# Held-back down products, more staging tiles, one conversion stream and a finer last norm in a fused attention and two-MoE kernel

## The chip, the cores and the metric

The kernel runs on 1 core of one Trainium2 chip. The metric is the device time of one execution in microseconds (us). Three timed runs of the kernel before gave 1191.64, 1191.96 and 1192.28 us; the median, 1191.96 us, is what a change is compared with. Times inside the kernel come from one profiled execution. PE is TensorE's matrix multiply, PEld its weight load, DVE is VectorE, ACT is ScalarE, POOL is GpSimd, and SP issues DMAs.

## What is computed

Three stages follow each other, on 6016 rows of 256 channels, all in float32:

```python
qn = q / (np.linalg.norm(q, axis=1, keepdims=True) + 1e-06)
kn = k / (np.linalg.norm(k, axis=1, keepdims=True) + 1e-06)
s = kn.transpose(0, 2, 1) @ qn / tau          # 256 x 256: attention over channels
a = softmax(s);  x = v @ a                    # 6016 x 256
h = np.maximum(x @ w_in, 0.0)                 # w_in 256 x 2048
x = h * h @ w_out                             # w_out 2048 x 256
xn = x / np.sqrt(np.mean(x * x, axis=-1) + 1e-06) * rms_g
g = xn @ w_gate;  val = xn @ w_val            # 256 x 1536 each
out = (g / (1 + np.exp(-g)) * val) @ w_out2   # 1536 x 256
```

## The kernel before

**Arithmetic.** A float32 operand is split into a high part (ACT, a copy that rounds) and a low part (DVE, a subtraction), and a product is three matmuls: high by high, low by high, high by low (`mm3`). The weights arrive in another number layout and are converted first: a `Call` scales halves on POOL and ACT (`a`, L142 and L145), then three DVE instructions put the bits together (`b0` L149, `b1` L153, `b2` L157), then `h` and `l` split the result.

**Stages.** The tokens lie in 12 blocks: 0 to 9 have 512 columns, 10 and 11 have 448. After the attention and the first weights (to 161 us), `mlp1` computes the first MoE for blocks 2 to 7, one block after another, 16 units a block: 6 matmuls up, relu and square on ACT and DVE, and 6 matmuls down that are held in `pending` until three units later. Blocks 8 and 9, and 10 and 11, are two pairs (4 and 5) for `mlp1_pair`: 8 groups of seven products of three matmuls each (A11, S1, S2, A12, S3, A22, S4), a scheme that needs seven products where a plain one needs eight. `mlp2` then does the second MoE for all six pairs the same way, 12 groups each.

**The pair stage, where most of the diff lies.** A group works in four PSUM banks. ACT copies a bank into the next one where a product adds on top of an earlier sum (`cp`, L1339 `bu` from `b0`, L1347 `bv` from `bu`), so a product may wait for ACT. Four results a group are relu'd and squared: for each, `square` makes a high part `sh` (`hi`, ACT, L1298), the full square (`full`, ACT L1302 or DVE L1304) and the low part (`lo`, DVE, L1307), and queues two down products (three matmuls each, lines 110 to 112, tiles `acc<-sh,wo_h`). They are put into the list `waiting` with the slot number from which they may go. Between the products there are eight calls of `down_slot` a group; a call issues what `pending` still holds from `mlp1`, and then the first down product of `waiting` that is due. `sh` lies in a rotating set of five buffers (`work`), and a group takes five. PE runs strictly in the order written, so a down product whose `sh` isn't ready stops the products behind it.

**Side work.** Beside the matmuls the kernel norms the finished blocks (`norm_steps`, `pair_norm`), splits them into seven operands and stores these in DRAM (`pair_steps`: `hi` L1038 on ACT, `lo` L1048 on DVE, a store from a staging tile after each), prepares the next pair's operands (`v_steps`), converts weights (`small_steps`, `stream`) and forms sums of `m` (`comb_steps`). In blocks 2 to 7 the tables `SKIP`, `ROWS` and `COMB` say which unit takes which step; in the pair stage and in `mlp2` a list `side` is taken off step by step by `aside`. Staging tiles are two buffers under the tag `ys`, for the last pair one `vt` and one `ys`. A step whose tile is still being stored waits, and with it everything behind it on ACT.

**Queues.** Nearly all DMAs go through SP's queue in the order written; `fetch` loads operands of `mlp2` back, `late_calls` load the last weights of w_out2 during `mlp2` and convert them, starting with the ACT step of L145.

Of the kernel before, what the change touches and what calls it, by code (L numbers as in the profile page):

```python
# [10 lines left out]
F32 = mybir.dt.float32  # L11
F32R = mybir.dt.float32r
# [16 lines left out]
def attn_moe_kernel(ctx: ExitStack, tc, q, k, v, tau, w_in, w_out, w_gate, w_val, w2, rms_g, out):  # L29
# [375 lines left out]
    def stream(cs, ahead):  # L405
# [8 lines left out]
        yield lambda: loads(ahead)  # L414
        for i, c in enumerate(cs):

            def bits(c=c):
                c.b0()
                c.b1()

            def whole(i=i, c=c):
                c.b2()
                if not c.keeps_raw:
                    loads(i + 1 + ahead)

            if i == 0:
                yield c.a
            yield from [bits, whole]
# [522 lines left out]
    def pair_norm(p):  # L951
# [64 lines left out]
        return [s1, s2, s2b, s3, s4, s5, s5b, s6(0), s6(1)]  # L1016

    def pair_steps(p, single=()):
# [3 lines left out]
        turn = []  # L1022
# [8 lines left out]
        def hi(i):  # L1031
            def f():
                if single:
                    st[i] = single[len(turn)][:, :, :n]
                    turn[:] = [] if turn else [0]
                else:
                    st[i] = xp.tile([P, 2, NB], F32R, tag="ys", name="xp", bufs=2)[:, :, :n]
# [15 lines left out]
        if single:  # L1053
            return sub, hi, lo

        def both(*fs):
# [5 lines left out]
            both(lo(6)),  # L1062
# [102 lines left out]
    def v_steps(p, into):  # L1165
# [11 lines left out]
        def tr(t, kk):  # L1177
            def f():
                if t == 0 and kk == 0:
                    st["t"] = vp.tile([P, KC, NB], F32, tag="vt", name="vt")[:, :, :n]  # L1180
                    st["a"], st["c"] = (place(k, F32)[:, :, :n] for k in (0, 1))
                    st["x"] = {
                        0: st["t"][:, 0], 4: st["t"][:, 1], 2: st["a"][:, 0], 6: st["a"][:, 1],
                        3: st["c"][:, 0], 1: st["c"][:, 1], 5: st["t"][:, 0],
                    }
# [54 lines left out]
    def through_dram(p):  # L1240

        count = [0]

        def into(i, n):
            if p not in v_dram:
                v_dram[p] = dp.tile([P, NC7, 2, NB], F32, tag=f"v{p}", name="vd")
            count[0] += 1
            t = place(6) if count[0] in (2, 4) else xp.tile([P, 2, NB], F32R, tag="ys", name="xp", bufs=2)
            t = t[:, :, :n]
# [19 lines left out]
    def mlp1_pair(p, ops, side, after_product, after_group):  # L1269
# [21 lines left out]
        def square(r, k, f, t, first, last):  # L1291
# [551 lines left out]
```

## Time and profile before

| | |
|---|---|
| timed runs, median | 1191.96 us (1191.64 to 1192.28) |
| the profiled execution | 1189.03 us, its span 1187.2 us |
| PE busy | 1137.5 us, 96% of the span, 5170 matmuls |
| PEld busy | 931.4 us, 78% |
| DVE busy, ACT busy | 777.5 us (65%), 789.9 us (67%) |
| POOL busy | 74.4 us (6%) |
| granted PE clock, mean | 0.993 |

The ends of matmuls are modelled in the profile: a matmul of 512 columns is shown with 389 ns, and the next one starts 227 ns after it when nothing is missing. So the busy share of PE says little about how dense it runs; the distance between starts, or the number of matmuls in a stretch, says it. A row in square brackets at the end of a timeline line is the engine's idle time before that instruction and what ended it.

### The profile page before, as it was taken

What the parts mean: (1) busy time and instruction counts of PE and PEld (TensorE: products, weight loads), DVE (VectorE), ACT (ScalarE), POOL (GpSimd) and SP (SyncE); (2) the same over time, 40 slices, a digit from 0 to 9 for tenths busy, and PEclk for the clock granted to TensorE, in tenths of its full rate; (3) what the DMA queues carried; (4) which work ended last, traced back from release to release, by engine and by line L of the source; (5) the groups of instructions that cost most, each with busy time, mean ns of one, the idle gap of its engine ahead of it and who ended that gap; (6) DMA issues with size and microseconds to landing.
All of it is one profiled execution on the core that took longest, in us unless ns stands there. A gap on an engine that the chain in (4) does not pass through costs nothing. (4 is left out here: it accounts for less than half of the span.)

```text
span 1187.2 us, 14551 instructions
## 1 busy us (share of the span) xinstructions
PE 1137.5 (96%) x5170; PEld 931.4 (78%) x5170; DVE 777.5 (65%) x1190; ACT 789.9 (67%) x1428; POOL 74.4 (6%) x106
## 2 busy tenths in 40 slices
PE   8999989999999998899888999999999999999997
PEld 7978878777778775667666778888888888888997
DVE  7998756688788775665653786655655655555655
ACT  7688768587788675666566776655655655655654
POOL 2421010210111000000000000000000000000000
PEclk9999999999999999999999999999999999999999
DMA  9533300363541310426034534202202201201101
GB/s 336 200 112 90 89 18 19 124 203 116 178 142 62 133 43 9 144 80 221 9 134 173 217 121 148 71 18 71 72 18 64 79 19 55 81 18 43 39 18 32
DMA packets 103033, 113.42 MB, mean 96 GB/s; under 512 B 50352, under 2 KB 71856, under 8 KB 102320
## 3 DMA queue, kind: packets, MB, share of 16 engines
q1 hardware_dynamic: 100688, 111.63, 28.3%
q10 hardware_dynamic: 2272, 0.85, 0.3%
q8 instruction: 41, 0.67, 0.2%
q14 instruction: 32, 0.26, 0.1%
HBM read 71.30 MB, written 41.16 MB: 95 GB/s over the span
## 5 line engine op out<-in xcount | busy, mean ns | idle before, releaser
L1414 PE MATMUL mm<-p,gv 128*128 128x512 f32 (+1 forms) x1188 | 304.1, 389 | 5.7 <-ACT mm L1456 4.7
L1414 PEld LDWEIGHTS mm<-p,gv 128*128 128x128 f32 x1188 | 222.3, 189 | 53.2 <-ACT mm L1456 6.3
L1505 DVE TENSOR_TENSOR sh<-hp,sh 128x512 fp32r<-128x512 f32 (+1 forms) x144 | 98.0, 681 | 144.7 <-ACT sh L1501 144.5
L111 PE MATMUL acc<-sh,wo_h 128*128 128x512 f32 (+1 forms) x384 | 155.4, 405 | 13.9 <-DVE sh L1307 11.3
L110 PE MATMUL acc<-sh,wo_h 128*128 128x512 f32 (+1 forms) x384 | 152.5, 397 | 9.9 <-ACT sh L1298 6.5
L112 PE MATMUL acc<-sh,wo_l 128*128 128x512 f32 (+1 forms) x384 | 150.0, 391 | 3.9 <-DVE wo_l L182 3.8
L1456 ACT COPY mm<-mm 128x512 f32<-128x512 f32 (+1 forms) x72 | 40.4, 562 | 168.6 <-PE mm L1414 163.6
L850 DVE TENSOR_TENSOR sh<-p,sh 128x512 fp32r<-128x512 f32 x128 | 92.1, 720 | 62.6 <-ACT sh L843 56.9
L110 PE MATMUL acc<-sh,w_h 128*128 128x512 f32 (+1 forms) x284 | 109.5, 386 | 0.0
L112 PE MATMUL acc<-sh,w_l 128*128 128x512 f32 (+1 forms) x284 | 109.5, 385 | 0.0
L111 PE MATMUL acc<-sh,w_h 128*128 128x512 f32 (+1 forms) x284 | 109.5, 385 | 0.0
L111 PEld LDWEIGHTS acc<-sh,wo_h 128*128 128x128 f32 x384 | 72.6, 189 | 43.9 <-DVE sh L1307 24.7
L110 PEld LDWEIGHTS acc<-sh,wo_h 128*128 128x128 f32 x384 | 72.5, 189 | 33.2 <-ACT sh L1298 14.3
L1501 ACT CAST sh<-hp 128x512 fp32r<-128x512 f32 (+1 forms) x144 | 88.9, 618 | 4.8 <-DVE hp L1515 2.8
L112 PE MATMUL mm<-p,m_l 128*128 128x512 f32 x224 | 87.8, 392 | 0.4 <-DVE m_l L774 0.4
L838 ACT ACTIVATE p<-mm 128x512 f32<-128x512 f32 x128 | 75.6, 591 | 18.7 <-PE mm L112 18.2
L110 PE MATMUL mm<-p,m_h 128*128 128x512 f32 x224 | 87.8, 392 | 0.2 <-ACT ns L929 0.2
L111 PE MATMUL mm<-p,m_h 128*128 128x512 f32 x224 | 87.5, 391 | 0.0
L112 PEld LDWEIGHTS acc<-sh,wo_l 128*128 128x128 f32 x384 | 72.7, 189 | 16.9 <-DVE wo_l L182 5.1
L1414 PE MATMUL mm<-xs,gv 128*128 128x512 f32 (+1 forms) x324 | 82.5, 381 | 0.0
L1489 DVE TENSOR_TENSOR hp<-mm,sg 128x512 f32<-128x512 f32 (+1 forms) x72 | 48.9, 680 | 42.9 <-PE mm L1414 42.7
L1414 PEld LDWEIGHTS mm<-xs,gv 128*128 128x128 f32 x324 | 60.8, 188 | 10.2
(245 smaller groups left out, 2072.5 us busy)
## 6 DMA issues: line engine op xcount, KB each, us to landing
xd<-xp SPq DMA_DIRECT2D x70, 256.0 KB, 2.1
p<-xd SPq DMA_DIRECT2D x58, 256.0 KB, 4.0
gv<-gvd SPq DMA_DIRECT2D x5, 1792.0 KB, 14.8
gvd<-gp SPq DMA_DIRECT2D x15, 512.0 KB, 3.1
raw<-in_moe_w_out_dram SPq DMA_DIRECT2D x10, 512.0 KB, 3.8
out_dram<-ot SPq DMA_DIRECT2D x40, 128.0 KB, 2.3
qraw<-in_q_dram SPq DMA_DIRECT2D x13, 384.0 KB, 7.2
qraw<-in_k_dram SPq DMA_DIRECT2D x13, 384.0 KB, 7.3
```

The costliest lines, as they stand in the source:

```text
L110: nc.tensor.matmul(o, wh, xh, start=start, stop=False)
L111: nc.tensor.matmul(o, wh, xl, start=False, stop=False)
L112: nc.tensor.matmul(o, wl, xh, start=False, stop=stop)
L838: nc.scalar.activation(out=r, in_=o, func=AF.Relu)
L850: nc.vector.tensor_tensor(out=sl, in0=s, in1=f32(sh), op=ALU.subtract)
L1414: nc.tensor.matmul(bank, c[:, hl, a, fs], x, start=start and j == 0, stop=j == 2, skip_group_check=not start)
L1456: cp(out=bu, in_=b0)
L1489: dve(out=h21, in0=bv, in1=sg1, op=ALU.mult)
L1501: nc.scalar.copy(out=parts[t][0], in_=x)
L1505: dve(out=pl, in0=x, in1=f32(ph), op=ALU.subtract)
```

## The change

The pair stage and the tables change, no matmul is added or removed:

- `square` takes a `lag`, and its down products are due `lag` slots later (3, 2, 3 and 4 for the four squares of a group; 0 before). `cp(out=bu)` goes ahead of the square left over from the group before, and the norm's matmul (`takes_bank`) ahead of two slots, in `mlp2` too.
- `staged(...)` gives `pair_steps` and `v_steps` tiles in turn: `ys, p0, ys, p1` (blocks 5 and 7, pair 5), `ys, p6, ys` (pair 4), `vt, ys` with both `ys` buffers (last pair), and two `ys` as before only in block 3. So that `p0` and `p1` are free for it, `v_steps` takes them later and the operands of `mlp2`'s first pair are fetched at group 6 of pair 5, not at group 1.
- The two conversion streams become one (`w2_calls + gv_calls`, two loads ahead), in which `b0`, `b1` and `b2` are one step; the tables spread the steps anew, and block 7 takes its steps at other units.
- `pair_norm`'s first step becomes two; the last pair's list starts with three steps of the norm, and the conversion of late weights comes fourth, where it was second.

```diff
-        def s1():
-            st["w"] = vp.tile([P, 2, NB], F32, tag="vraw", name="w") if last else place(2, F32)
-            st["q"] = xp.tile([P, 2, NB], F32, tag="ys", name="q", bufs=2)
-            for d, x in enumerate((st["w"], st["q"])):
-                nc.scalar.activation(out=halves(x), in_=both(d), func=AF.Square)
+        def s1(d):
+            def f():
+                if d == 0:
+                    st["w"] = vp.tile([P, 2, NB], F32, tag="vraw", name="w") if last else place(2, F32)
+                    st["q"] = xp.tile([P, 2, NB], F32, tag="ys", name="q", bufs=2)
+                nc.scalar.activation(out=halves(st["wq"[d]]), in_=both(d), func=AF.Square)
+
+            return f
...
+    def staged(*tags):
+
+        turns = cycle(tags)
+
+        def tile():
+            t = next(turns)
+            if t[0] == "p":
+                return place(int(t[1]))
+            pool, k = (xp, 2) if t == "ys" else (vp, 1)
+            return pool.tile([P, 2, NB], F32R, tag=t, name="xp", bufs=k)
+
+        return tile
...
-                waiting.extend((slots["n"], down(f, t, d, st["h"], st["l"], first, last)) for d in range(KC))
+                due = slots["n"] + lag
+                waiting.extend((due, down(f, t, d, st["h"], st["l"], first, last)) for d in range(KC))
...
+            cp(out=bu, in_=b0)
             if old:
                 old[0]()
                 old[1](False)
                 old[2]()
-            cp(out=bu, in_=b0)
...
-            hi, full, lo = square(rx[:, 0], 0, f0, 0, first, False)
+            hi, full, lo = square(rx[:, 0], 0, f0, 0, first, False, 3)
...
+            if side and getattr(side[0], "takes_bank", False):
+                side.pop(0)(b0)()
             down_slot()
             down_slot()
-            if side and getattr(side[0], "takes_bank", False):
-                side.pop(0)(b0)()
             aside()
-            hi, full, lo = square(rx[:, 1], 1, f1, 1, first, False)
+            hi, full, lo = square(rx[:, 1], 1, f1, 1, first, False, 2)
...
-            hi, full, lo = square(ry[:, 0], 0, f1, 0, False, last)
+            hi, full, lo = square(ry[:, 0], 0, f1, 0, False, last, 3)
...
-            left.append(square(ry[:, 1], 1, f0, 1, False, last))
+            left.append(square(ry[:, 1], 1, f0, 1, False, last, 4))
...
-    conv = chain(small_steps(), stream(gv_calls, NRAW - 1))
-    conv2 = stream(w2_calls, 1)
+    conv = chain(small_steps(), stream(w2_calls + gv_calls, NRAW - 1))
...
-                if g == 1:
-                    for i in ORDER[:2]:
-                        fetch(0, i, ops0)
                 if g == NF1 // 2 - 2:
                     assert not side, len(side)
-                    fetch(0, 1, ops0)
+                    for i in ORDER[:3]:
+                        fetch(0, i, ops0)
...
     side = []
+    side += pair_side[:3]
+    del pair_side[:3]
     for i in range(max(len(rows_steps), len(pair_side))):
-        side += pair_side[i : i + 1] + rows_steps[i : i + 1]
+        side += rows_steps[i : i + 1] + pair_side[i : i + 1]
```

What this does to the order is seen on the engines (line numbers of the changed kernel are those of its own file: L1321 there is L1316, L1302 there is L1298). First PE, in the first group of pair 4 (`vr,m_h` are the products A12 and, later, A22; `vr,c3` is S3; `acc<-sh` are down products of the group's own squares), before:

```order
L1316 MATMUL mm_4002<-vr_3792,m_h_758 128x512
L110 MATMUL acc0_4056<-sh_4052,wo_h_91 128x512
L111 MATMUL acc0_4056<-sh_4052,wo_h_91 128x512
L112 MATMUL acc0_4056<-sh_4052,wo_l_92 128x512
L1316 MATMUL mm_4005<-vr_3949,c3_3622 128x512
L1316 MATMUL mm_4005<-vr_3949,c3_3623 128x512
L1316 MATMUL mm_4005<-vr_3949,c3_3622 128x512
L110 MATMUL acc1_4065<-sh_4052,wo_h_91 128x512
```

and now:

```order
L1321 MATMUL mm_4002<-vr_3785,m_h_758 128x512
L1321 MATMUL mm_4005<-vr_3924,c3_3622 128x512
L1321 MATMUL mm_4005<-vr_3924,c3_3623 128x512
L1321 MATMUL mm_4005<-vr_3924,c3_3622 128x512
L1321 MATMUL mm_4005<-vr_3970,m_h_758 128x512
L1321 MATMUL mm_4005<-vr_3970,m_l_759 128x512
L1321 MATMUL mm_4005<-vr_3970,m_h_758 128x512
L110 MATMUL acc0_4073<-sh_4050,wo_h_91 128x512
```

Three slots of this first group stay empty, and the first down products move behind A22; from there on every slot is filled, with down products that are older. In a later group of pair 4 ACT's rows name the squares (`sh<-p3` is first the square of A12's result, then that of S3's), before:

```order
L1351 ACTIVATE p3_3999<-mm_4279 128x512
L1298 ACTIVATE sh_4323<-p3_3999 128x512
L1358 COPY sh_4313<-mm_4282 128x512
L1038 CAST xp_4343<-xst_3783 128x512
L1298 ACTIVATE sh_4346<-p3_3999 128x512
```

and now:

```order
L1356 ACTIVATE p3_3999<-mm_4271 128x512
L1302 ACTIVATE sh_4315<-p3_3999 128x512
L1363 COPY sh_4305<-mm_4274 128x512
L1048 CAST xp_4335<-xst_3821 128x512
L1302 ACTIVATE sh_4338<-p3_3999 128x512
```

and PE's rows of the same group show which of them is read behind A22, before:

```order
L1316 MATMUL mm_4282<-vr_3990,m_l_759 128x512
L1316 MATMUL mm_4282<-vr_3990,m_h_758 128x512
L110 MATMUL acc0_4083<-sh_4346,wo_h_91 128x512
L111 MATMUL acc0_4083<-sh_4346,wo_h_91 128x512
L112 MATMUL acc0_4083<-sh_4346,wo_l_92 128x512
```

and now:

```order
L1321 MATMUL mm_4274<-vr_3970,m_l_759 128x512
L1321 MATMUL mm_4274<-vr_3970,m_h_758 128x512
L110 MATMUL acc0_4073<-sh_4315,wo_h_91 128x512
L111 MATMUL acc0_4073<-sh_4315,wo_h_91 128x512
L112 MATMUL acc0_4073<-sh_4315,wo_l_92 128x512
```

Behind A22 the down product of the newest square (`sh_4346`) stood; now that of the square before it (`sh_4315`) stands there, and the newest one moves to the next group's first slots. Third, ACT at the end of `mlp2`'s first group and in its second (`w<-xst` and `q<-xst` are the norm's first step, `pu<-pu` the late weights' conversion, `mm<-mm` the copies that products need), before:

```order
L975 ACTIVATE w<-xst 128x896
L975 ACTIVATE q<-xst 128x896
L145 ACTIVATE pu<-pu 128x512
L1456 COPY mm<-mm 128x512
L1501 CAST sh<-hp 128x512
L1512 ACTIVATE sg<-sg 128x512
```

and now:

```order
L975 ACTIVATE w<-xst 128x896
L975 ACTIVATE q<-xst 128x896
L1461 COPY mm<-mm 128x512
L1506 CAST sh<-hp 128x512
L1517 ACTIVATE sg<-sg 128x512
L1476 COPY mm<-mm 128x512
L1477 COPY pu<-mm 128x512
L1506 CAST sh<-hp 128x512
L1481 ACTIVATE sg<-mm 128x512
L1485 COPY pu<-mm 128x512
L145 ACTIVATE pu<-pu 128x512
L1461 COPY mm<-mm 128x512
```

The conversion `pu<-pu` stood right behind `q<-xst`, ahead of the copy `mm<-mm` of the second group; now that group's copies come first.

## Rows read from the trace of the kernel before

**Rows 1.** Stretches: us, busy time (x count) of PE, PEld, DVE, ACT, POOL; clock, DMA.

```profile
161.27:439.14 277.87, 270.84 (x1167) 217.63 (x1166) 207.77 (x316) 214.36 (x380) 36.48 (x44) 0.99 0.33 109
439.14:545.00 105.86, 93.80 (x369) 67.97 (x368) 66.43 (x106) 65.64 (x117) 0.00 (x0) 0.98 0.26 92
545.00:638.06 93.06, 82.80 (x364) 66.88 (x362) 54.30 (x87) 57.23 (x108) 0.00 (x0) 0.98 0.26 95
638.06:699.79 61.73, 56.37 (x236) 44.22 (x235) 41.73 (x68) 43.12 (x79) 2.04 (x4) 0.97 0.50 194
699.79:1092.70 392.91, 392.53 (x1730) 323.68 (x1729) 228.35 (x345) 235.96 (x445) 0.65 (x1) 1.00 0.19 60
...
1103.00:1173.00 70.00, 70.00 (x346) 64.48 (x345) 40.79 (x68) 40.90 (x86) 0.00 (x0) 1.00 0.06 16
```

**Rows 2.** Waits of weight loads, 439.14 to 638.06: total us, times, longest.

```profile
PEld acc L111 <- DVE sh L1307: 24.7, 46, 1.4
PEld acc L110 <- ACT sh L1298: 14.3, 19, 2.0
PEld mm L1316 <- ACT mm L1339: 3.8, 3, 2.7
PEld mm L1316 <- ACT mm L1347: 2.5, 2, 2.1
```

**Rows 3.** Timeline of PE, pair 4: start, us, instruction, count, idle before.

```profile
503.67 0.84 PE L1316 MATMUL mm<-vr,c 128*128 128x512 f32 x3
504.51 0.49 PE L110 MATMUL acc<-sh,wo_h 128*128 128x512 f32 x1
505.40 0.50 PE L111 MATMUL acc<-sh,wo_h 128*128 128x512 f32 x1 [0.40 <-DVE sh L1307]
```

**Rows 4.** Timeline of ACT in the same group.

```profile
503.19 0.60 ACT L1351 ACTIVATE p<-mm 128x512 f32<-128x512 f32 x1 [0.28 <-PE mm L1316]
503.82 0.63 ACT L1298 ACTIVATE sh<-p 128x512 fp32r<-128x512 f32 x1
```

**Rows 5.** Timeline of DVE in the same group.

```profile
504.65 0.69 DVE L1307 TENSOR_TENSOR sh<-p,sh 128x512 fp32r<-128x512 f32 x1
```

**Rows 6.** A stretch of pair 4's first group, columns as in rows 1.

```profile
454.00:457.00 3.00, 3.00 (x8) 2.31 (x8) 0.99 (x2) 0.86 (x3) 0.00 (x0) 0.50 0.00 0
```

**Rows 7.** Waits of ACT for DMAs over the whole span.

```profile
ACT xp L1038 <- DMA xd<-xp: 21.8, 13, 3.5
ACT raw L145 <- DMA raw<-in_moe_w_out_dram: 7.8, 1, 7.8
```

**Rows 8.** Timeline of PE: single waits in blocks, pairs and the start of `mlp2`.

```profile
219.27 0.49 PE L110 MATMUL acc<-sh,wo_h 128*128 128x512 f32 x1 [1.09 <-ACT sh L843]
...
411.92 0.50 PE L110 MATMUL acc<-sh,wo_h 128*128 128x512 f32 x1 [1.38 <-ACT sh L846]
...
426.56 0.37 PE L925 MATMUL mm<-ns,mean_w 128*128 128x16 f32 x2 [1.20 <-DVE ns L919]
...
491.03 0.96 PE L1316 MATMUL mm<-vr,c 128*128 128x512 f32 x3 [1.64 <-ACT mm L1347]
...
596.64 0.47 PE L1316 MATMUL mm<-vf,ch 128*128 128x448 f32 x1 [2.34 <-ACT mm L1339]
...
645.40 3.09 PE L1414 MATMUL mm<-p,gv 128*128 128x512 f32 x12 [0.67 <-ACT pu L1480]
652.12 3.85 PE L1414 MATMUL mm<-p,gv 128*128 128x512 f32 x9 [3.64 <-ACT mm L1456]
```

**Rows 9.** Timeline of ACT at the late weights' first conversion.

```profile
650.92 0.67 ACT L145 ACTIVATE pu<-pu 128x512 int32<-128x512 uint32 x1 [3.88 <-DMA pu<-in_moe_w_out_dram]
```

**Rows 10.** Groups of DVE, 161.27 to 439.14: count, busy us, mean ns, idle before.

```profile
L153 DVE CUSTOM_DVE_ANT_0 dg<-raw,dg 128x1024 uint16<-128x1024 uint16 x13 | 9.0, 692 | 0.4
L157 DVE SCALAR_TENSOR_TENSOR dg<-raw,dg 128x512 int32<-128x512 int32 x13 | 8.8, 678 | 0.0
L149 DVE TENSOR_SCALAR dg<-dg 128x512 int32<-128x512 int32 x13 | 5.9, 451 | 0.5 <-POOL dg L142 0.5
```

More of the change, by code (lines that the diff above doesn't have):

```diff
@@ L1 @@
 from contextlib import ExitStack
-from itertools import chain
+from itertools import chain, cycle
 import concourse.bass as bass
@@ L412, in loads, with first @@
                 done[0] += 1
-        yield lambda: loads(ahead)
+        def first():
+            upto("h", len(calls))
+            upto("l", len(calls))
+            loads(ahead)
+        yield from [first, lambda: None, cs[0].a]
         for i, c in enumerate(cs):
-            def bits(c=c):
-                c.b0()
-                c.b1()
             def whole(i=i, c=c):
-                c.b2()
+                c.b()
                 if not c.keeps_raw:
                     loads(i + 1 + ahead)
-            if i == 0:
-                yield c.a
-            yield from [bits, whole]
+            yield whole
             hl = c.hl_steps()
@@ L1032, in f @@
             def f():
[L1033 to L1037, printed above, removed]
+                st[i] = stage()[:, :, :n]
                 nc.scalar.copy(out=st[i][:, 0], in_=xst[p][:, i, :n])
@@ L1179, in f @@
                 if t == 0 and kk == 0:
[L1180 to L1185, printed above, removed]
+                    x = vp.tile([P, KC, NB], F32, tag="vt", name="vt")[:, :, :n]
+                    st["x"] = {0: x[:, 0], 4: x[:, 1], 5: x[:, 0]}
+                if t == 1 and kk == 0:
+                    a, c = (place(k, F32)[:, :, :n] for k in (0, 1))
+                    st["x"].update({2: a[:, 0], 6: a[:, 1], 3: c[:, 0], 1: c[:, 1]})
                 x = st["x"][SLOT[t][kk]]
@@ L1240, in through_dram @@
     def through_dram(p):
-        count = [0]
+        tile = staged("ys", "p6", "ys", "p6", "ys", "ys", "ys")
         def into(i, n):
@@ L1246, in into @@
                 v_dram[p] = dp.tile([P, NC7, 2, NB], F32, tag=f"v{p}", name="vd")
[L1247 to L1249 removed]
+            t = tile()[:, :, :n]
             return t[:, 0], t[:, 1], lambda: nc.sync.dma_start(out=v_dram[p][:, i, :, :n], in_=f32(t))
@@ L1289, in down, with square @@
             return g
-        def square(r, k, f, t, first, last):
+        def square(r, k, f, t, first, last, lag):
             st = {}
@@ L1481, in group @@
             add(out=h22, in0=bh, in1=w, op=ALU.add)
+            if side and getattr(side[0], "takes_bank", False):
+                side.pop(0)(b0)()
             down_slots()
             down_slots()
-            if side and getattr(side[0], "takes_bank", False):
-                side.pop(0)(b0)()
             if f:
@@ L1684, in attn_moe_kernel @@
         if b == CONV[-1]:
-            left = [len(list(x)) for x in (conv, conv2, cstep)]
-            assert left == [0, 0, 0] and state["b"] == len(calls) == state["l"], left
+            left = [len(list(x)) for x in (conv, cstep)]
+            assert left == [0, 0] and state["b"] == len(calls) == state["l"], left
     assert not spill
@@ L1708, in after_group @@
             if g == 0:
-                side.extend((pair_norm(p - 1) + pair_steps(p - 1) if p > FIRST else []) + ([] if last else v_next[2:]))
+                side.extend((pair_norm(p - 1) + pair_steps(p - 1, staged("ys", "p0", "ys", "p1")) if p > FIRST else []) + ([] if last else v_next[2:]))
             if not last and g == NF1 // 2 - 2:
@@ L1727, in attn_moe_kernel @@
         ops1 = nxt
-    stage = [pool.tile([P, 2, NB], F32R, tag=t, name="xp", bufs=k) for pool, t, k in ((vp, "vt", 1), (xp, "ys", 2))]
-    sub, hi, lo = pair_steps(NP - 1, stage)
     silu_table()
```

40 lines of the change are left out of this document (13 added, 27 removed).

## The prediction, made before the change was run

> **What bounds the kernel now.** Read the stretches first [rows 1]. From 699.79 to 1092.70 us, inside `mlp2`, 1730 matmuls of 512 columns start in 392.91 us: 0.2271 us each, with no wait; for 448 columns 346 take 70.0 us, 0.2023 each. These are the price of a matmul when PE never waits, and with them the other stretches show what PE loses. Blocks 2 to 7 hold 6 x 192 = 1152 matmuls: 277.87 - 261.6 = 16.2 us lost. Pair 4 holds 8 x 45, plus 18 down products left by block 7, less 12 that run over: 366 x 0.2271 = 83.1, so 105.86 - 83.1 = 22.7 lost. Pair 5: 12 x 0.2271 + 348 x 0.2023 = 73.1 of 93.06, 19.9 lost. The start of `mlp2`, 220 of 512 and 12 of 448: 52.4 of 61.73, 9.3 lost. (The counts of the rows are a few higher, for matmuls that reach over an edge and the norm's tiny ones.) So PE bounds nearly everything, and 68.1 us are holes that can be closed; what lies before 161 us isn't touched.
>
> Here a page reads differently. PE's busy column leaves only 12.1 and 10.3 us idle in the two pairs, 22.3 against the 42.6 counted above [rows 1]. The Trainium skill (Perfetto Trace Analysis, Identifying the Most-Contended Engine) calls matmul busy share a poor measure because pipelined matmuls mislead in the trace, and wants the share of weight loads instead. That share is 323.68 of 392.91, 82.4%, in the dense stretch and 64.48 of 70.00, 92.1%, for 448 columns; at these the loads of the pairs, 67.97 and 66.88, would take 82.5 and 72.6 us, 43.8 us less than they do. By the busy column the pairs could give 20 us less than I forecast; the trace sides with the page.
>
> **What the holes in the pairs are.** The waits of the weight loads name them [rows 2]: 24.7 us for the low part `sh` of DVE L1307, 14.3 for the high part of ACT L1298, and only 3.8 and 2.5 for ACT's copies of banks. So 39.0 of 45.7 us, some 36 of the 42.6, are down products that stand on PE before their square is done. One group shows how [rows 3 to 5]: S3 starts at 503.67 and takes 3 x 0.227; the down product behind it, due at 504.35, starts its first matmul at 504.51 and its second at 505.40. The square it needs came from A12's result: relu at 503.19, high part at 503.82, low part from 504.65. A12 had ended one down product before S3, at 502.99, so to that second matmul the chain takes 2.4 us; PE has six matmuls, 1.36 us, to do meanwhile.
>
> **The part that holds down products back.** With lags of 3, 2, 3, 4 and eight slots for eight products a group, the order settles so: the square of A12 is used behind A22, 15 matmuls or 3.4 us after A12's end (2.4 needed); that of S3 in the next group's first slot, behind 21 matmuls after S3 or 4.8 us; the two others 24 or more matmuls after their products. In a group with no side work nothing is left to wait for. I check that the engines can follow: in pair 4 DVE has 66.43 and ACT 65.64 us of work for a dense 83.1 us (80 and 79%), in pair 5 54.30 and 57.23 for 73.1 [rows 1]. No engine becomes the bound on average. What stays: the first group of pair 4, where three slots are empty and S3 and A22 follow A12 without cover. ACT then has two copies of block 7's results, relu, high part and the copy behind S3, five times about 0.6 us [rows 4], some 3.2 us with hand-overs where PE has 1.36: 1.8 us lost. The clock may fall there too: in the same group before, behind two waits on squares, it stood at 0.50 (1.2 GHz) from 454.00 to 457.00, and eight matmuls took 0.2 us longer each, 1.6 us [rows 6]; half of that is counted. Five groups a pair carry side steps; counted from the order at 0.6 to 0.7 us an instruction [rows 4, 5], they come to 7 to 9.7 us on the fuller engine, against 10.2 of matmuls in pair 4 and 9.1 in pair 5; no row shows such a group at full speed. Bounds are 0, as in groups without, and 2 us each; I take 0.5, nearer to the first, since a copy has 2 us of cover. Pair 4 keeps 1.8 + 0.8 + 2.5, with the rounding up 5.5, pair 5 2.5: 8 of 42.6 stay, 34.6 gained.
>
> On the fall of the clock the Trainium skill (Perfetto Trace Analysis, Matmul Optimizations) says that TensorE scales with its utilization and wants matmuls back to back in batches. That speaks against leaving slots empty; the rows above show such a fall in this very group already. With it in full the sum is 0.8 us worse, without it 0.8 us better.
>
> **The part that stages in more tiles.** ACT waited 13 times, 21.8 us in all, for a store out of a staging tile [rows 7], while the tile's next user comes one or two steps later. Three of these waits reached PE: at 411.92 in block 7 (1.38 us idle before a high part, then a low part, then matmuls at the low clock; by the starts 4.1 us over the dense price), at 491.03 (1.64 idle) and at 596.64 (2.34, then nine matmuls at the low clock) [rows 8]. The last two are within the 42.6. With three or four tiles a tile's next user comes two or more steps later than now, and the wait is covered. Behind the wait in block 7 stood the norm, and the 1.20 at 426.56 (1.4 with the next matmul) [rows 8] goes with it, as far as a step moved by one unit lets it. Block 3 keeps two tiles.
>
> **The conversions.** The other ACT wait on a DMA, 7.8 us [rows 7], is the first of the rows of w_out2: loaded one step ahead behind a store on SP; PE lost 2.3 us after it, by 1.09 idle at 219.27 [rows 8] and smaller waits around it. In the single stream it is loaded two steps ahead with no store in front. Block losses named so far: 4.1 + 1.4 + 2.3 = 7.8 of 16.2. The remaining 8.4 comes from units with too many steps at once, and the tables only shuffle these. Fewer steps means L149, L153 and L157 in one unit, 0.45 + 0.69 + 0.68 = 1.8 us on DVE where 1.1 and 0.7 stood in two, 13 times [rows 10], and behind them in DVE's order waits the next unit's low part. PE reads it three units (8.2 us) later, so a single such clump is covered; two engines late at once are not. The 8.4 could become 3 or 17; I take 8.0. Gain 8.2.
>
> **The last norm.** At 652.12 PE had waited 3.64 us, and with the low clock after it lost 5.7, for a copy on ACT that stood behind L145 [rows 8]. L145 had waited 3.88 us for its load, which landed at 650.92 [rows 9]. Now L145 stands behind the second group's copies. The first group's 41 matmuls, dense, end at some 647.1, the second group's S3 21 matmuls or 4.8 us later, and the copy behind it near 652.6, after the landing. The first group lost another 0.67 idle at 645.40 [rows 8] behind S3, where now two held products stand as cover. 9.3 becomes 2.6: gain 6.7. Fetching the first operands at group 6 leaves two groups, 18 us, for them: nothing. Splitting the norm's first step adds no instruction.
>
> **Sum.** 34.6 + 8.2 + 6.7 = 49.5. On the profiled execution's own 1189.03 that is 1139.5; the median of the runs lies 2.9 above that execution, so 1142.5.
>
> **Rivals.**
> *The waits move to ACT and DVE.* Both are in order, and a denser PE brings their work closer. For it: ACT is at 79% and each group has several hand-overs. Against: the dense stretch of `mlp2`, the same scheme with products held two slots, waits for nothing at 60% ACT. Half of the pairs' holes, 21 us, would stay, and the blocks' 16.2 too: 1142.5 + 13 + 8.2 = 1163.7. Chance 0.12.
> *The clumped conversions cost more than the tiles save.* Each of 13 clumps holds the next low part by 0.7 us and more; if each passes 1.2 us on to PE, 15.6 is added to blocks that gain nothing: 1142.5 + 8.2 + 15.6 = 1166.3. For it: the 8.4 us that full units cost already. Against: three units of cover. Chance 0.07.
> *It doesn't do what it says.* The products are moved, but what they wait for moves with them, because the squares start later behind the copies. Then the 36 us stay, and only tiles, conversions and norm give: 1142.5 + 36 - 8 = 1170. Against: cp and squares keep their places within a few 0.6 us steps. Chance 0.03.
> *Slower: the held products keep `sh` occupied.* Five buffers, five taken a group: each square takes the buffer of the same square a group earlier. If a buffer were still held, the high part on ACT would wait, and in order behind it the copies that products need. At one product and one down, 1.36 us, for each of four squares in 16 groups, 87 us: 1229.5. It decides once a held product stands behind the point of reuse; the closest, A22's square, is freed 12 matmuls (2.7 us) before that. Chance 0.03.
>
> **How the numbers follow.** The forecast has 0.75 and its own range, from the bounds above, is 1131 (pairs keep 2, blocks 3) to 1160 (pairs 18, blocks 16). The range 1131 to 1163 takes in that and the nearer part of the first rival and leaves some 2 in 10 out. Faster by over 0.2% (2.4 us, about what a measurement of this kernel can tell) 0.96, slower 0.03, within 0.01.
>
> **What would show it.** Pair 4 some 88 us long and pair 5 some 76; waits of weight loads for `sh` near zero; no wait over 2 us of ACT for a staging store beyond block 3; blocks 2 to 7 near 270; L145 late in `mlp2`'s second group and no half clock there. It is wrong if groups without side work stay over 10.4 us, or if ACT's copies become the waits.

## The result, and the profile after

The changed kernel takes **1135.73 us** (median of 4 runs, 1134.87 to 1137.26); the kernel before, run beside it, 1192.12 (1191.64 to 1195.30). The ratio is 0.9523, with a 95% interval of 0.9504 to 0.9542. The prediction was 1142.5 with a range of 1131 to 1163, so the time fell inside it, 6.8 us under the forecast. The profiled execution took 1137.26 us, its span 1135.3.

In the code after, the lines that matter have moved a little: the pairs' products are L1321 (L1316 before), the squares' high part L1302 (L1298), the low part L1311 (L1307), the two bank copies L1340 and L1352 (L1339, L1347), the copy behind S3 L1363 (L1358), the staging copy L1048 (L1038), the products of `mlp2` L1419 (L1414), their first copy L1461 (L1456).

The stretches that answer to [rows 1], in the same order and columns: blocks 2 to 7, pair 4, pair 5, the start of `mlp2`, and its dense part.

```profile
157.62:426.72 269.10, 266.04 (x1167) 219.62 (x1166) 207.91 (x315) 216.81 (x378) 31.93 (x41) 0.99 0.34 115
426.72:511.27 84.55, 83.09 (x363) 67.40 (x362) 65.78 (x105) 64.32 (x118) 0.15 (x1) 1.00 0.29 103
511.27:588.05 76.78, 74.97 (x363) 67.62 (x362) 54.04 (x87) 55.57 (x107) 0.00 (x0) 1.00 0.34 125
588.05:649.80 61.75, 59.49 (x255) 46.34 (x254) 45.31 (x72) 45.46 (x84) 2.36 (x4) 1.00 0.54 206
649.90:1040.00 390.10, 390.10 (x1721) 322.17 (x1720) 226.02 (x341) 233.93 (x442) 0.97 (x1) 1.00 0.19 59
```

Pair 4 went from 105.86 to 84.55 us, pair 5 from 93.06 to 76.78, with nearly the same busy time on DVE and ACT as before (ACT 1.3 and 1.7 us less): PE has all but stopped waiting for these two engines. Six matmuls of pair 4, 1.4 us, now run behind it, and six of pair 5 run in the start of `mlp2`. The dense part costs what it did: 390.10 us over 1721 matmuls is 0.2267 each.

The waits of the weight loads over both pairs, 426.72 to 588.05 (what waited, for what: total us, times, longest), against 24.7, 14.3, 3.8 and 2.5 us in [rows 2]:

```profile
PEld mm L1321 <- ACT sh L1363: 2.0, 3, 1.6
PEld mm L1321 <- ACT mm L1340: 2.0, 2, 1.7
PEld mm L1321 <- ACT mm L1352: 1.1, 2, 0.7
PEld acc L111 <- DVE sh L1311: 0.9, 1, 0.9
```

The down products' waits for squares are gone but for one. And ACT's waits for stores out of staging tiles over the whole span, 21.8 us in [rows 7]; the wait of L145 for the rows of w_out2, 7.8 us there, no longer appears:

```profile
ACT xp L1048 <- DMA xd<-xp: 5.1, 7, 1.4
```

To compare many kernels I use one measure on each one's trace: over all matmuls of 512 or 448 columns in a stretch, how much later the next matmul starts than 0.2271 us (512) or 0.2023 us (448) after this one, summed. That is PE's loss, idle time and slow clock together. Distances behind smaller matmuls are left out, so the first row holds nothing of the attention (to 61.8 us). The start of `mlp2` is the same 253 matmuls in every kernel.

| PE's loss, us, in | before | after | change |
|---|---|---|---|
| ahead of block 2 (to 157.62 us; before: to 161.27) | 6.2 | 2.5 | -3.7 |
| blocks 2 to 7 | 15.2 | 6.2 | -9.0 |
| pair 4 | 22.6 | 2.7 | -19.9 |
| pair 5 | 20.0 | 3.6 | -16.4 |
| start of `mlp2` | 9.5 | 4.9 | -4.6 |
| behind it | 0.4 | 1.7 | +1.3 |
| sum | 73.9 | 21.6 | -52.3 |

The span became 51.9 us shorter, so this table holds the whole difference. Two of its rows weren't in the prediction: the first and the last.

### The profile page after: what moved, and what is told of

The parts are those of the page before. It is cut to its first block, busy times and chain, and to the rows that moved or that the text cites. A ratio compares the mean times of both kernels' runs of the same rounds, so it can differ in the third digit from the quotient of the medians.

```text
span 1135.3 us, 14564 instructions
## 1 busy us (share of the span) xinstructions
PE 1115.5 (98%) x5170; PEld 934.6 (82%) x5170; DVE 778.1 (69%) x1190; ACT 789.9 (70%) x1428; POOL 70.9 (6%) x106
## 4 chain that ended last, share of the span: by engine, by line
PE 83%; DVE 5%; ACT 5%; DMA 2%; issue 2%; POOL 1%; SPq 0%; DVEq 0%; ACTq 0%; POOLq 0%
PE mm L1419 28%; PE acc L110 12%; PE acc L112 12%; PE acc L111 12%; PE mm L1321 6%; PE mm L110 4%; PE mm L111 4%; PE mm L112 4%; POOL rows L569 1%; DMA qraw<-in_k_dram 1%; DMA rraw<-in_v_dram 1%; PE mm L761 1%; DMA xd<-xp 1%; ACT sh L842 0%; ACT p L841 0%
## 5 line engine op out<-in xcount | busy, mean ns | idle before, releaser
L1419 PE MATMUL mm<-p,gv 128*128 128x512 f32 (+1 forms) x1188 | 303.4, 388 | 2.0 <-ACT mm L1461 1.6
L1419 PEld LDWEIGHTS mm<-p,gv 128*128 128x128 f32 x1188 | 221.4, 188 | 49.7 <-ACT mm L1461 3.0
L1461 ACT COPY mm<-mm 128x512 f32<-128x512 f32 (+1 forms) x72 | 40.4, 562 | 171.9 <-PE mm L1419 144.5
L111 PE MATMUL acc<-sh,wo_h 128*128 128x512 f32 (+1 forms) x384 | 149.2, 389 | 0.6 <-DVE sh L1311 0.5
L110 PE MATMUL acc<-sh,wo_h 128*128 128x512 f32 (+1 forms) x384 | 149.7, 390 | 0.0
L1419 PE MATMUL mm<-xs,gv 128*128 128x512 f32 (+1 forms) x324 | 82.9, 382 | 0.0
L1419 PEld LDWEIGHTS mm<-xs,gv 128*128 128x128 f32 x324 | 60.9, 188 | 10.5
```

The lines of the kernel that those rows point to most:

```text
L110: nc.tensor.matmul(o, wh, xh, start=start, stop=False)
L111: nc.tensor.matmul(o, wh, xl, start=False, stop=False)
L1419: nc.tensor.matmul(bank, c[:, hl, a, fs], x, start=start and j == 0, stop=j == 2, skip_group_check=not start)
L1461: cp(out=bu, in_=b0)
```

## Experiments

Each median is over 4 to 10 runs, set beside runs of the kernel before (medians 1191.5 to 1192.1, single runs 1189.2 to 1200.7). Not all kernels ran on the same chip, so a difference of a microsecond or two between two medians isn't told by them alone. The columns of the losses are those of the table above, from one profiled run of each kernel.

| kernel | median us | ahead | 2 to 7 | pair 4 | pair 5 | `mlp2` start |
|---|---|---|---|---|---|---|
| before | 1192.12 | 6.2 | 15.2 | 22.6 | 20.0 | 9.5 |
| before, products held back | 1164.59 | 7.8 | 16.5 | 7.6 | 9.0 | 8.1 |
| before, last w_out conversion finished early | 1187.77 | 2.4 | 14.9 | 23.9 | 19.8 | 10.0 |
| after | 1135.73 | 2.5 | 6.2 | 2.7 | 3.6 | 4.9 |
| after, nothing held back | 1165.38 | 2.4 | 6.4 | 18.2 | 16.1 | 6.4 |
| after, all held by one slot | 1140.97 | 2.4 | 5.8 | 5.1 | 5.7 | 5.7 |
| after, all held by two slots | 1137.37 | 2.4 | 6.6 | 2.9 | 2.9 | 4.9 |
| after, two staging tiles | 1146.60 | 2.4 | 7.3 | 6.9 | 8.0 | 4.8 |
| after, copy of bu second | 1137.42 | 2.4 | 6.5 | 3.2 | 3.4 | 5.5 |
| after, old order at the start of `mlp2` | 1138.76 | 2.4 | 6.0 | 2.7 | 2.9 | 10.1 |
| after, without the clearing on POOL | 1131.93 | 2.4 | 1.7 | 2.7 | 3.6 | 5.2 |
| that, side steps of pair 5 spread | 1128.72 | 2.4 | 1.8 | 2.7 | 0.5 | 5.1 |
| that, and the start of `mlp2` spread | 1127.93 | 2.4 | 1.7 | 2.7 | 0.4 | 3.6 |

**Nothing held back** (after, undone):

```diff
-            hi, full, lo = square(rx[:, 0], 0, f0, 0, first, False, 3)
+            hi, full, lo = square(rx[:, 0], 0, f0, 0, first, False, 0)
...
-            left.append(square(ry[:, 1], 1, f0, 1, False, last, 4))
+            left.append(square(ry[:, 1], 1, f0, 1, False, last, 0))
```

> The kernel after with the four lags set to 0, all else as changed. Theory (the hold-back gives the pairs' gain): PE waits again for ACT L1302 and DVE L1311 in nearly every group, as in [rows 2], so pairs 4 and 5 last 25 to 36 us longer and the whole 1161 to 1172 us. Rival (the freed ACT and DVE steps, the third tile and the copy of bu ahead of the old square give it): the pairs stay within 5 us of the kernel after, 1136 to 1141 us.

Measured: 1165.38 us (ratio to before 0.9765, 0.9733 to 0.9798), 29.7 slower than after. The waits of the weight loads in its pairs (427.21 to 618.5) are those of [rows 2] again:

```profile
PEld acc L111 <- DVE sh L1311: 27.1, 49, 1.4
PEld acc L110 <- ACT sh L1302: 9.8, 17, 1.8
PEld mm L1321 <- ACT mm L1340: 1.1, 2, 0.8
```

The theory holds, and the rival (freed steps, third tile, copy order) falls as the main cause: with all of these in place PE still stands 36.9 us at the squares. The pairs lose 28.0 us more than in after. But they lose 34.3 us here and 42.6 before, so 8.3 us of their gain came without any hold-back.

**The hold-back alone** (before, with lags 3, 2, 3 and 4 added, and nothing else):

```diff
-                waiting.extend((slots["n"], down(f, t, d, st["h"], st["l"], first, last)) for d in range(KC))
+                due = slots["n"] + lag
+                waiting.extend((due, down(f, t, d, st["h"], st["l"], first, last)) for d in range(KC))
```

> The kernel before with lags of 3, 2, 3 and 4 slots and nothing else. Theory: the two pairs lose 10 us or less in place of 42.6, so 25 to 34 us are gained and the time is 1158 to 1167 us, with blocks 2 to 7 as they were. Rival (the cover is only useful with the new staging and order): under 15 us of gain, 1177 us or more.

Measured: 1164.59 us (0.9765, 0.9736 to 0.9795), 27.5 faster than before. But the pairs lose 16.6 us, not the 10 or less that I expected. Its waits in the pairs (441.91 to 614.2), in lines close to those of before (L1340 and L1348 are the two bank copies):

```profile
PEld mm L1317 <- ACT mm L1340: 6.0, 4, 3.6
PEld mm L1317 <- ACT mm L1348: 4.3, 3, 2.9
PEld mm L1317 <- ACT sh L1359: 2.0, 3, 1.6
PEld acc L111 <- DVE sh L1307: 1.2, 2, 0.8
```

The squares' 39.0 us are 1.2, as in after. In their place the waits for ACT's bank copies grew from 6.3 us in [rows 2] to 10.3. The two longest stand at products where PE waited before as well (491.03 and 596.64 in [rows 8], for 1.64 and 2.34 us), and ahead of each copy ACT stands for a store out of a staging tile:

```profile
482.44 0.62 ACT L1038 CAST xp<-xst 128x512 fp32r<-128x512 f32 x1 [1.98 <-DMA xd<-xp]
574.26 0.62 ACT L1038 CAST xp<-xst 128x512 fp32r<-128x512 f32 x1 [3.03 <-DMA xd<-xp]
```

```profile
483.60 0.66 PE L1317 MATMUL mm<-vr,c 128*128 128x512 f32 x1 [2.52 <-ACT mm L1348]
575.84 0.68 PE L1317 MATMUL mm<-vf,ch 128*128 128x448 f32 x1 [3.27 <-ACT mm L1340]
```

In the kernel before ACT stood there for 1.96 and 3.53 us. The store's wait hasn't grown; PE, no longer held up by squares, comes to the copy earlier. So part of the copies' lateness lay under waits for squares. (The 1.6 us more ahead of block 2 are a fall of the clock behind the same wait as before; see the last section.)

**Two staging tiles** (after, undone for all pairs but the last):

```diff
-            x = pair_steps(b // 2 - 1, staged("ys") if b == 3 else staged("ys", "p0", "ys", "p1"))
+            x = pair_steps(b // 2 - 1, staged("ys"))
```

and the same at the two other calls of `pair_steps` ahead of the last pair's.

> The kernel after with the operands of pairs 3, 4 and 5's inputs staged in the two old tiles alone. Theory by the prediction's sum (4.1 us of block 7, and part of what pairs 4 and 5 and the start of mlp2 lost to a late tile): 4 to 10 us slower than after, 1140 to 1146 us, with ACT waiting for DMA queues at the staging copies again as in [rows 7]. Rival (with fewer conversion steps the two tiles come free in time): within 1.5 us of after.

Measured: 1146.60 us (1146.03 to 1147.87), 10.9 slower than after, a little over what I expected. ACT's waits for stores over the whole span are those of [rows 7] again:

```profile
ACT xp L1048 <- DMA xd<-xp: 21.6, 15, 3.1
```

and the weight loads of the pairs (427.82 to 598.5) wait for the bank copies that stand behind it on ACT:

```profile
PEld mm L1321 <- ACT mm L1340: 5.2, 3, 3.2
PEld mm L1321 <- ACT mm L1352: 5.1, 3, 2.9
PEld mm L1321 <- ACT sh L1363: 2.3, 4, 1.6
PEld acc L111 <- DVE sh L1311: 0.8, 1, 0.8
```

The first three lines are nearly those of the hold-back alone, at the same two products. So the 8.6 us that the pairs lose more here are what the tiles are worth with the hold-back in place, about the 8.3 that the first experiment left over; in blocks 2 to 7 they are worth 1.1.

**All held by one slot** (after, and so for the other three lags):

```diff
-            hi, full, lo = square(rx[:, 0], 0, f0, 0, first, False, 3)
+            hi, full, lo = square(rx[:, 0], 0, f0, 0, first, False, 1)
```

> The kernel after with all four lags at 1. Theory (the chain from A12 needs 2.4 us, and with this lag its square is used 9 matmuls, 2.0 us, after A12's end, and that of S3 behind 9 matmuls too, S4's side square behind one product): 0.4 to 0.5 us are missing in each of 15 groups, so 6 to 8 us slower than after, 1142 to 1144 us. Rival (any cover is enough once the products are no longer first in line): within 2 us of after. A third view (half of the cover, half of the gain of the hold-back): 13 to 15 us slower.

Measured: 1140.97 us (1140.69 to 1141.01), 5.2 slower, just under the theory's range. The pairs' waits (426.41 to 593.5):

```profile
PEld acc L111 <- DVE sh L1311: 10.0, 20, 1.0
PEld acc L110 <- ACT sh L1302: 1.5, 3, 1.1
```

The pairs lose 4.5 us more, 0.30 in each of 15 groups. The chain's 2.4 us less the 2.04 us of nine matmuls is 0.36, or 5.4 in all; I had rounded it up to 0.4 and 0.5. So the chain's length decides, not the mere fact of a delay.

**All held by two slots:**

```diff
-            hi, full, lo = square(rx[:, 0], 0, f0, 0, first, False, 3)
+            hi, full, lo = square(rx[:, 0], 0, f0, 0, first, False, 2)
```

> The kernel after with all four lags at 2: in all groups but the first of pair 4 the slots come out as with 3, 2, 3, 4, and in that first group a product stands ahead of A22. Theory (the 1.3 us stall of that group is A22 following S3 without cover): 0.5 to 1.5 us faster, 1134.2 to 1135.2 us. Rival (the product that is put there isn't ready itself, 6 matmuls and 1.4 us after A12): the same stall, within 0.3 us of after, or up to 1 us slower.

Measured: 1137.37 us (1136.46 to 1137.82), 1.6 slower than after, outside both expectations but with ranges that overlap, and no stretch of its trace is worse by over 0.4. The stall of the first group is not cured, it is shared out (timeline of PE: start, length, instruction, idle time before in brackets; first this kernel, then after):

```profile
435.31 0.84 PE L1321 MATMUL mm<-vr,c 128*128 128x512 f32 x3
436.82 0.51 PE L110 MATMUL acc<-sh,wo_h 128*128 128x512 f32 x1 [0.67 <-ACT sh L1302]
437.71 0.50 PE L111 MATMUL acc<-sh,wo_h 128*128 128x512 f32 x1 [0.39 <-DVE sh L1311]
```

```profile
433.71 0.84 PE L1321 MATMUL mm<-vr,c 128*128 128x512 f32 x3
435.70 0.50 PE L1321 MATMUL mm<-vr,m_h 128*128 128x512 f32 x1 [1.14 <-ACT sh L1363]
```

In after, A22 waits for the copy behind S3; with a product in between, that product waits for its own square. The theory falls and the rival's mechanism holds: what is put there isn't ready either. Where the 1.6 us of the medians come from isn't shown. From the starts the two waits cost 1.50 us, the one 1.30.

**The copy of bu second** (after, undone):

```diff
-            cp(out=bu, in_=b0)
             if old:
                 old[0]()
                 old[1](False)
                 old[2]()
+            cp(out=bu, in_=b0)
```

> The kernel after with the copy of bank bu behind the old square's high part again, as in before; hold-back and staging stay. Theory (in before PE waited 3.8 us for this copy, L1339 in [rows 2], and a high part of 0.6 us ahead of it on ACT takes most of the cover that one product of S1 and two held ones, 9 matmuls or 2.0 us, leave): 1 to 4 us slower, 1137 to 1140 us. Rival (9 matmuls cover two ACT steps of 0.6 us): within 0.7 us of after.

Measured: 1137.42 us (1137.37 to 1138.92), 1.7 slower; the pairs lose 6.6 us in place of 6.3, the start of `mlp2` 0.6 more. The median is inside the theory's range, but the trace shows only a part of it in the pairs. This edit is worth a microsecond or so, and can't be told from nothing with certainty.

**The hole ahead of 161 us** (before, one edit in the stream of conversions):

```diff
-        yield lambda: loads(ahead)
+        def first():
+            upto("h", len(calls))
+            upto("l", len(calls))
+            loads(ahead)
+
+        yield first
```

> The kernel before, with the last w_out conversion finished in the first step of the stream of gate conversions in place of the step after next. Theory (the 3.63 us that PE waits for DVE L182 at 152 us is that conversion standing behind three DVE steps of the stream): 2.5 to 4 us faster than before, 1188 to 1189.6 us, and no PE wait over 1 us at 152 us. Rival (PE would wait there for something else, a transfer or an ACT step): within 1 us of before.

Measured: 1187.77 us, 4.4 faster (ratio 0.9955, 0.9934 to 0.9976), a little under the expected range; in the trace PE loses 3.8 us less ahead of block 2. This is the hole in the kernel before, on PE and then on DVE:

```profile
148.21 0.39 PE L111 MATMUL acc<-sh,wo_h 128*128 128x512 f32 x1
152.08 0.50 PE L112 MATMUL acc<-sh,wo_l 128*128 128x512 f32 x1 [3.47 <-DVE wo_l L182]
```

```profile
148.02 0.42 DVE L149 TENSOR_SCALAR dg<-dg 128x512 int32<-128x512 int32 x1
148.48 0.69 DVE L153 CUSTOM_DVE_ANT_0 dg<-raw,dg 128x1024 uint16<-128x1024 uint16 x1
150.13 0.69 DVE L850 TENSOR_TENSOR sh<-p,sh 128x512 fp32r<-128x512 f32 x1 [0.95 <-ACT sh L843]
150.74 0.68 DVE L157 SCALAR_TENSOR_TENSOR dg<-raw,dg 128x512 int32<-128x512 int32 x1
151.34 0.68 DVE L182 TENSOR_TENSOR wo_l<-dg,wo_h 128x512 fp32r<-128x512 f32 x1
```

The low part of the last w_out piece, L182, is written only when its reader asks for it, behind three steps of the next stream on DVE. With the edit it runs here, 8 us earlier, and PE passes without a wait:

```profile
143.13 0.69 DVE L182 TENSOR_TENSOR wo_l<-dg,wo_h 128x512 fp32r<-128x512 f32 x1
```

The changed kernel's merged stream begins with the same step (`first`, a part that the diff above leaves out), and there L182 runs early too. I had read that step as book-keeping.

```profile
142.70 0.69 DVE L182 TENSOR_TENSOR wo_l<-dg,wo_h 128x512 fp32r<-128x512 f32 x1
```

**The old order at the start of `mlp2`** (after, undone):

```diff
-    side += pair_side[:3]
-    del pair_side[:3]
...
-        side += rows_steps[i : i + 1] + pair_side[i : i + 1]
+        side += pair_side[i : i + 1] + rows_steps[i : i + 1]
```

with the norm's two squares in one step again.

> The kernel after with the old order of side steps at the start of mlp2 (both squares of the norm in one step, then L145 ahead of the second group's copies). Theory: in after the load for L145 lands at 600.8 us, the second group's first copy runs at 598.2; with L145 ahead of it that copy is 2.6 + 0.7 us late, and the clock falls behind it as in [rows 8], so 3 to 5 us slower than after, 1138.7 to 1140.7 us. Rival (the copies have slack in a group that starts with cover from held products): under 1.5 us slower.

Measured: 1138.76 us (1138.62 to 1139.92), 3.0 slower; the stretch itself loses 5.2 us more, and after's own profiled run lost 2 us more than this one elsewhere. On ACT L145 waits for its load again, the copy L1461 behind it comes late, and so does PE:

```profile
600.73 0.66 ACT L145 ACTIVATE pu<-pu 128x512 int32<-128x512 uint32 x1 [3.50 <-DMA pu<-in_moe_w_out_dram]
601.29 0.58 ACT L1461 COPY mm<-mm 128x512 f32<-128x512 f32 x1
```

```profile
601.93 4.21 PE L1419 MATMUL mm<-p,gv 128*128 128x512 f32 x9 [3.60 <-ACT mm L1461]
```

The granted clock from 602 to 604 us was 0.50. The prediction's mechanism for this part is the right one.

**The hole that the change brought.** In after, most of what blocks 2 to 7 still lose is one place in block 4. The timelines of PE, DVE and POOL there:

```profile
254.53 0.40 PE L112 MATMUL mm<-p,m_l 128*128 128x512 f32 x1
257.85 0.58 PE L924 MATMUL mm<-ns,mean_w 128*128 128x16 f32 x2 [2.93 <-DVE ns L918]
```

```profile
253.13 0.69 DVE L157 SCALAR_TENSOR_TENSOR dg<-raw,dg 128x512 int32<-128x512 int32 x1
257.02 0.69 DVE L918 TENSOR_REDUCE ns<-p 128x16 f32<-128x512 f32 x1 [3.20 <-POOL ns L882]
```

```profile
253.99 0.74 POOL L297 TENSOR_TENSOR raw<-dg 128x256 f32<-128x256 f32 x1 [8.53 <-DVE dg L157]
...
256.17 0.72 POOL L300 TENSOR_TENSOR raw<-dg,raw 128x256 f32<-128x256 f32 x1
256.83 0.15 POOL L882 MEMSET ns<- 128x64 f32 x1
```

PE waits for the norm's reduction on DVE, that for a clearing of 0.15 us on POOL, and that stands behind four additions, L297 to L300, of the conversion whose three DVE steps are now one step and end just before, at 253.82. So POOL, 6% busy, sets the end of this wait. DVE stood for 3.20 us, and with it the next low part; from 258 to 264 us the clock was at 0.53 in the mean. By the starts of the matmuls all of it is 6.4 us (6.0 in the table's measure, which leaves out the norm's two tiny matmuls). The Trainium skill (Perfetto Trace Analysis, Tensor Engine Instruction) says that ACT, DVE and GpSimd take their instructions strictly in order; the trace agrees: nothing behind the reduction ran on DVE in those 3.20 us. In the kernel before, with the three DVE steps still apart, the reduction once met the same burst of additions, which L157 alone releases:

```profile
172.77 0.69 DVE L919 TENSOR_REDUCE ns<-p 128x16 f32<-128x512 f32 x1 [1.53 <-POOL ns L883]
```

There three other DVE steps lay between L157 and the reduction, the wait was half as long, and PE ran through it densely. So the hole isn't shown to come from making three steps one; what differs is that now nothing stands between L157 and the reduction. The edit leaves the clearing out:

```diff
         x = norm_small.tile([P, 2, 2 * NB // 32], F32, tag="ns", name="ns")
-        if G < 2 * NB // 32:
-            nc.gpsimd.memset(x, 0.0)
```

> The kernel after without the clearing of the norm's small tile on POOL (the reduction writes every column that is read later, so nothing of the result is left out). Theory (the 6.4 us hole at 257.9 us in block 4 is DVE's reduction waiting for that clearing behind four additions on POOL, with a fall of the clock behind it): the hole goes and the time is 5.0 to 6.5 us shorter, 1129.2 to 1130.7 us. Rival (the norm's matmul would wait there all the same, since DVE is the engine that is full): under 2 us shorter.

Measured: 1131.93 us (1130.64 to 1133.01; ratio to before 0.9491, 0.9468 to 0.9513), 3.8 faster than after by the medians. Blocks 2 to 7, and PE where the hole was:

```profile
156.94:421.23 264.29, 263.19 (x1168) 217.74 (x1166) 209.81 (x315) 216.17 (x378) 33.23 (x35) 1.00 0.35 117
```

```profile
255.78 0.50 PE L111 MATMUL acc<-sh,wo_h 128*128 128x512 f32 x1 [1.10 <-DVE sh L849]
```

The stretch is 4.8 us shorter, and of the hole one wait of 1.10 us is left, for DVE, full at that moment. I had expected 5.0 to 6.5, and the 3.8 lies between that and the rival's under 2: the wait that stays (1.34 us by the starts) is the share that the rival had right.

**Side steps spread.** In after, 1.49 us of pair 5's loss are one wait: PE at 553.30 for a copy on ACT, behind a staging copy that waited 1.56 us for a subtraction on DVE, one group after both scalings of `xst`, 2.48 us, stood on DVE from 543.72. Pair 5 has room for empty side steps, since no operands are made for a next pair:

```diff
+                x = pair_norm(p - 1) + pair_steps(p - 1, staged("ys", "p0", "ys", "p1")) if p > FIRST else []
+                if last:
+                    x = [f for k, s in enumerate(x) for f in [s] + [lambda: None] * (k in REST)]
```

with `REST` = 5 and 7 to 13.

> The kernel without the clearing, and in pair 5 eight empty side steps, so that the side steps stand alone. Theory (the 1.49 and 0.64 us of PE's waits in pair 5 are the two scalings of xst, 1.24 us each on DVE, in one group, with the subtraction for the next high part behind them): pair 5 loses some 1.2 us in place of 3.6, so 2 to 2.5 us faster than without the clearing alone, 1129.4 to 1130 us. Rival (the wait moves to the next group with steps): within 0.7 us of that kernel's 1131.9.

Measured: 1128.72 us (1128.51 to 1129.09; 0.9468, 0.9445 to 0.9492), 3.2 faster than without the clearing alone. Pair 5, whose row in after was 76.78 us with PE busy for 74.97:

```profile
506.81:581.12 74.31, 74.31 (x365) 68.14 (x364) 55.08 (x88) 56.45 (x108) 0.00 (x0) 1.00 0.33 120
```

PE never idles in it. The gain is over the expected 2 to 2.5, since nearly all of the 3.6 went. Which of the eight empty steps does it was not tried, so the two scalings as the cause are argued from the trace.

**The start of `mlp2` spread as well**, with two empty steps behind the norm's matmul:

```diff
     pair_side = pair_norm(NP - 1) + pair_steps(NP - 1, staged("vt", "ys"))
+    pair_side[6:6] = [lambda: None] * 2
```

> As the kernel with the spread steps in pair 5, and two empty side steps behind the last norm's matmul at the start of mlp2, so that L145 and the copy of 896 columns leave the group in which ACT loads its tables twice (1.28 us each). Theory: of the 5.2 us lost there 1.0 to 1.6 go, 1128 to 1129 us. Rival (all later steps move by half a group, and a copy there meets L145 as before): within 0.7 us of the kernel with pair 5 alone changed.

Measured: 1127.93 us (1127.26 to 1130.16; 0.9464, 0.9442 to 0.9486). The stretch loses 3.6 us in place of 5.1, as expected, but the medians are 0.8 apart and the ranges overlap: no more than likely. It has the lowest median of all, 7.8 us under the changed kernel.

## Why the prediction came out as it did

**The bound.** PE's losses were rightly sized: 68.1 us counted as holes that could be closed, of which 50 closed. The sentence that failed is "what lies before 161 us isn't touched": 3.7 us went there, through the first step of the merged stream, as the edit to before showed. The counts had been taken from 161 us on; PE's wait of 3.47 us ahead of that was not among them.

The reading by the share of weight loads stands. PE's busy column gave the pairs 22.3 us of idle time before and 3.3 after, 19 gained; the pairs became 37.6 us shorter. The Trainium skill (Perfetto Trace Analysis, Identifying the Most-Contended Engine) calls the busy share of matmuls a poor measure and names the share of weight loads, beside one of FLOPs, as a better one. The trace agrees: that share went from 64.2 to 79.7% in pair 4 and from 71.9 to 88.1% in pair 5, near the 82.4 and 92.1% of the dense stretches.

**The hold-back, 34.6.** The pairs gained 36.3, but the step that put all of it to the held products is wrong in its parts. Alone they give 26.0 in the pairs; the tiles, on top of them, give 8.6. The prediction said that "some 36 of the 42.6" were waits for squares, from the totals in [rows 2]. When these are taken away, PE comes earlier to ACT's bank copies behind late stores, and waits there longer: 6.3 us before, 10.3 with the hold-back alone. The total came out right in part by luck: the prediction counted waits for squares as gained whole, and the tiles, from which it expected only two waits in the pairs to go, removed what came out from under them. The chain of 2.4 us from [rows 3 to 5] was right: 2.04 us of cover left 0.30 us a group, 3.4 us left none in the groups without side work.

Pair 4's first group: 1.8 + 0.8 predicted, 1.30 measured, with the clock at 1.00 throughout (433 to 440 us); it fell in the same group before, behind two waits. The Trainium skill (Perfetto Trace Analysis, Matmul Optimizations) wants matmuls back to back in batches; the idle 1.14 us at 435.70 that the empty slots leave showed no effect on the clock in this trace. The 0.5 us a group for side steps: 0.3 in pair 4, from what it lost beyond its first group (1.2 us over four groups); in pair 5 0.7 over five, but most of it is one wait of 1.49 and one of 0.65.

**Tiles and conversions in blocks 2 to 7, 8.2.** The loss fell by 9.0: the right size by luck, since the steps are wrong. "The remaining 8.4 comes from units with too many steps at once, and the tables only shuffle these" fails on both sides. The old holes nearly all went; 6.4 us came new, where a conversion's end releases four additions on POOL right ahead of the clearing; without the clearing 1.7 are left. The prediction looked for a clump's harm at the low part behind it on DVE, and not at POOL. How much of the old holes the single stream closed and how much the new tables, no run tells apart. Of the staging's 4.1 in block 7 the two-tile kernel shows 1.1.

**The last norm, 6.7.** Measured 4.6: the mechanism is right (the old order brings back 5.2 us, the wait for the load and the half clock), but "9.3 becomes 2.6" left out that the displaced steps land in other groups of ACT's: waits of 0.96 us at 623.06 and 647.73, 0.53 at 635.28.

**The 2.9 from profile to median.** The profiled run of after lies 1.5 above its median, not 2.9 below. These 4.4 us are the largest piece of the 6.8. The sum itself gave 1139.5 for the profiled execution, which took 1137.26: 3.7 ahead of 161 us, 1.7 in the pairs, 0.8 in the blocks, less 2.1 at the last norm and 1.3 behind it, make 2.8 by the table, against 2.2 between the two figures. So errors of both signs stand behind the small distance.

**The rivals.** That the waits move to ACT and DVE is wrong for the kernel as it is, but right for the hold-back alone, on a small scale. And the sign against the prediction that it named, ACT's copies becoming the waits, is there in small: of the 6.0 us of waits listed for the pairs after, 5.1 are for such copies (L1363, L1340, L1352). That clumped conversions cost as much as the tiles save: blocks 2 to 7 became 8.8 us shorter, and the one large hole of 6.4 us came by way of POOL, not by thirteen late low parts of 1.2. That it does nothing is excluded by the run with nothing held back, 29.7 slower than after; and for occupied `sh` buffers no wait of ACT shows.

## What to carry to other kernels

A wait's total says how long PE stood, not what taking its cause away gains: ask which second wait PE would come to next, behind the first, and price both together. When steps on one engine are moved, follow all that they release, also onto an engine that is nearly idle: a tiny instruction there that a busy engine waits for stands behind the whole burst. And count the waits of the entire span before setting a part of it aside as untouched, since an edit to a work list's first step moves what came before it too.

## What the runs showed of the hardware

An instruction of 0.15 us on POOL stood at the end of a chain that cost PE 6.4 us, by three queues in order and a fall of the clock behind the wait; without it blocks 2 to 7 were 4.8 us shorter.

When the clock falls isn't told by the length of a wait. The clearest case is one and the same wait, for L182 at 152 us, in two kernels that are equal up to there: 3.47 us in the kernel before (152.08), and 3.48 in that with the hold-back alone (151.98). Behind it the clock stayed at 1.00 in the one execution and fell to 0.50, the lower of the two levels (1.2 GHz of 2.4), in the other. The rows have the columns of [rows 1], first before, then the hold-back alone:

```profile
153.00:156.00 3.00, 3.00 (x15) 2.48 (x14) 0.69 (x1) 1.29 (x3) 0.00 (x0) 1.00 0.49 164
```

```profile
153.00:156.00 3.00, 3.00 (x9) 2.32 (x8) 0.00 (x0) 0.00 (x0) 0.00 (x0) 0.50 0.47 162
```

Behind shorter waits it also went either way. Behind single waits of 1.14 us (435.70 in after) and 1.33 us (553.30) it stayed at 1.00, and so it did behind 0.67 and 0.39 us with one matmul between them (all held by two slots). In the kernel before it fell to 0.50 behind 0.60 and 0.74 us with one matmul between (452.46 and 453.71, ahead of [rows 6]; 1.35 and 0.39 us had passed idle at 447.90 and 448.79), and to 0.51 behind 1.38 and 0.39 us (411.92 and 412.81). In after it fell behind 2.93 us, in the old order at the start of `mlp2` behind 3.60. What decides is left open.
